# The last batch of a Fourier layer with routed experts: two queues for its loads, ACT's queue for its stores, and the last two experts' steps in plain order

## The chip, the cores and the metric

The kernel runs on one core of a Trainium2 chip. The metric is the device time of one execution in microseconds (us). TensorE is called PE in the rows (PEld is its weight load), VectorE DVE, ScalarE ACT, GpSimd POOL, SyncE SP; PEq, SPq, ACTq and POOLq are the sequencers of these engines, which issue DMA transfers. Each engine takes its own instructions in the order in which they stand in the program.

## The reference

For 8 batches of a 3136 x 256 sequence, a spectral layer is applied, and then a small expert network to the 128 rows of each batch that score highest.

```
X = rfft(x, axis=1)                       # 8 x 3136 x 256
Yr = Xr @ w_r - Xi @ w_i + b_r
Yi = Xr @ w_i + Xi @ w_r + b_i
Y = softshrink(Yr, 0.01) + 1j * softshrink(Yi, 0.01)
y = irfft(Y, n=3136, axis=1)

scores = y @ w_gate                       # 8 x 3136
for b in range(8):
    top = the 128 rows of y[b] with the highest scores[b]
    h = relu(y[b, top] @ w1)              # w1: 256 x 1024
    ye = h @ w2                           # w2: 1024 x 256
    out[b, top] = y[b, top] + sigmoid(scores[b, top])[:, None] * ye
    out[b] elsewhere = y[b]
```

## The kernel before

The transform of length 3136 is done as 98 x 32. For each batch there are five stages, all of them matmuls: `s1` (the 98-point transform; its result goes to a DRAM scratch tensor `As`), `s2` (the 32-point transform with twiddles), `spectral` (the product with the weights and the shrinkage), `s2i` (the inverse 32-point transform; its result goes to a DRAM scratch tensor `Cs`) and `s1i` (the inverse 98-point transform, whose result is the output row block). The stages of neighbouring batches run interleaved in one long loop over `t`. `s1i` runs in 16 steps a batch, `i` = 0 to 15. Two steps share one load of 98 x 1024 numbers (392 KB) from `Cs`, done by `ld_c`, and one store of the same size to `out`. For batches 0 to 6 the loaded rows are split into two parts on ACT and POOL (`split_c`, tiles `ch` and `cl`); batch 7 uses the rows as they are in one matmul (tiles `cv`, `xt` and `av`, after the three pools that its eight loads borrow). A PE result of `s1i` is copied by ACT from PSUM (tile `s`) to an SBUF tile called `ot` (two buffers) or, for some groups of batch 7, `at` (three buffers), and the store reads that tile. All of these loads and stores are issued from SP's queue. The eight loads of batch 7 are issued together, as soon as `Cs` of batch 7 is written.

Beside this runs the routing. `score` forms a batch's scores. `select` finds the 128th highest score: twelve rounds for batch 7, each of which counts on DVE (tiles `c`, `n`), sums over partitions on PE (line 258), and takes the next digit on DVE (tiles `ok`, `d`, `w`, `f`). `place` makes the list of the chosen rows (`mask`, `mt`, `row`, `hot`, and at last `idx`). Then the expert steps of one batch follow:

- `gather` (L327): POOL fetches the 128 rows of `out[b]` by an indirect DMA into `xe`. It waits until all stores of `out[b]` have landed.
- `prepare` (L335 to L343): PE transposes `xe`, DVE copies the result to `xT` (L337) and forms the gate's sum `sg` (L340), ACT takes the sigmoid `ga`.
- `hidden` (L352 to L356): 16 matmuls in two halves of 8. Each half ends in `hh` (ACT, L355) and `hl` (DVE, L356).
- `combine` (lines 227 to 229, 366 and 367): 24 matmuls into a tile named `px` (for the last batches), `ye` on DVE, and an indirect DMA on POOL that writes the 128 rows to `out[b]` (the scatter).

`fetch` and `ffn` are generators that are advanced once in each step of the loop; `fetch` runs at most two batches ahead of `ffn`. In `ffn` the last two batches are treated specially: for batch 6 the rows of batch 7 are prepared between `hidden` and `combine`, for which `ffn` waits until batch 7's `gather` has been called:

```
            if e == B * NCHK - 2:
                while len(fetched) < 2:
                    yield
                ready = prepare(*fetched[1], "m")
            combine(*item, ga, hs, tags[0])
```

The code above gives what is done; a scheduler decides the order of the instructions on each engine, and waits are placed on semaphores where data or a buffer asks for it. So an edit in one place can change the order in another.

## Time and profile before

| | |
|---|---|
| median of 3 runs | 760.71 us (760.18 to 762.15) |
| the profiled execution, its own time | 762.52 us |
| span in that execution, first to last instruction | 760.8 us |
| mean granted clock of TensorE | 0.989 |
| busy, share of the span | PE 97%, DVE 69%, ACT 64%, POOL 47% |

Times in the rows are microseconds from the start of the span. A row of a timeline gives start, duration, engine, line, operation, what it writes and reads, shape, and count; in brackets stands how long the engine had been idle before it and which event ended the wait. A PE matmul on unsplit 32-bit operands (L335, L352, L520) is shown as two passes, so "x32" there are 16 matmuls.

### The profile page before, as it was taken

The numbers are of one execution on the slowest core, as the hardware profiler recorded it, in microseconds if no ns is written. First come the engines' busy times: TensorE is split into PE (matmuls) and PEld (weight loads), VectorE is DVE, ScalarE is ACT, GpSimd is POOL, SyncE is SP. The second block draws the span as 40 slices with busy tenths as digits, with TensorE's granted clock in tenths as the row PEclk, the third lists the DMA queues.
The fourth block names the chain that finished last, engine by engine and source line by source line (L and its number), as shares of the span: only waits on it lengthen the run. The fifth ranks groups of instructions, "written<-read, shape, count | busy, mean of one in ns | idle before, by whom it ended". The sixth has DMA issues, their size and how long they took to land.

```text
span 760.8 us, 14956 instructions
## 1 busy us (share of the span) xinstructions
PE 736.0 (97%) x5232; PEld 652.9 (86%) x5232; DVE 522.5 (69%) x1413; ACT 488.1 (64%) x994; POOL 357.2 (47%) x372
## 2 busy tenths in 40 slices
PE   8799999999999999999999999999999999999987
PEld 3499989998999899999998888888999888988567
DVE  3267766665666656655898898776787799886652
ACT  2257656777787867777777768677577555455421
POOL 0345536556566655556466555565453332333101
PEclk9899999999999999999999999999999999999988
DMA  8989877888887888678767768576674364343830
GB/s 257 293 254 284 246 235 232 304 242 266 258 258 237 268 247 250 221 255 243 250 207 253 226 206 269 181 256 194 181 229 142 128 204 141 109 145 110 253 130 22
DMA packets 86224, 165.19 MB, mean 217 GB/s; under 512 B 6369, under 2 KB 58757, under 8 KB 86149
## 3 DMA queue, kind: packets, MB, share of 16 engines
q1 hardware_dynamic: 83534, 157.40, 66.1%
q0 software_dynamic: 2160, 5.60, 2.6%
q10 hardware_dynamic: 454, 1.25, 0.6%
q8 instruction: 41, 0.67, 0.4%
q14 instruction: 35, 0.28, 0.1%
HBM read 86.17 MB, written 78.12 MB: 216 GB/s over the span
## 4 chain that ended last, share of the span: by engine, by line
PE 79%; DVE 9%; DMA 6%; issue 3%; ACT 2%; POOL 0%; SPq 0%; POOLq 0%; ACTq 0%; DVEq 0%
PE py L227 11%; PE py L229 11%; PE py L228 11%; PE px L437 11%; PE s L229 9%; PE s L227 9%; PE s L228 9%; PE m L352 2%; DMA out<-ot 2%; PE s L410 2%; DMA As<-at 1%; DMA av<-As 1%; DMA xt<-in_x 1%; DVE junk L482 1%; DVE w L271 1%
## 5 line engine op out<-in xcount | busy, mean ns | idle before, releaser
L223 POOL TENSOR_TENSOR cl<-cv,ch 98x512 fp32r<-98x512 f32 x112 | 144.3, 1289 | 187.4 <-ACT ch L221 133.2
L223 POOL TENSOR_TENSOR xl<-xt,xh 98x512 fp32r<-98x512 f32 x112 | 144.4, 1291 | 92.3 <-ACT xh L221 80.3
L478 ACT COPY ct<-s 128x512 f32<-128x512 f32 (+1 forms) x104 | 59.3, 570 | 161.4 <-PE s L229 148.4
L227 PE MATMUL py<-wrh,Xh 128*128 128x256 f32 x400 | 121.8, 305 | 0.7 <-ACT Xh L440 0.7
L437 PEld LDWEIGHTS px<-g_sb,av 128*128 128x128 f32 (+1 forms) x800 | 106.3, 194 | 18.0 <-issue 5.6
L437 PE MATMUL px<-g_sb,av 128*128 128x128 f32 (+1 forms) x800 | 109.9, 280 | 4.6 <-DMA av<-As 4.2
L229 PE MATMUL py<-wrl,Xh 128*128 128x256 f32 x400 | 113.6, 284 | 0.0
L227 PE MATMUL py<-wih,Xh 128*128 128x256 f32 x400 | 113.2, 283 | 0.0
L228 PE MATMUL py<-wrh,Xl 128*128 128x256 f32 x400 | 113.2, 283 | 0.0
L228 PE MATMUL py<-wih,Xl 128*128 128x256 f32 x400 | 113.1, 283 | 0.0
L229 PE MATMUL py<-wil,Xh 128*128 128x256 f32 x400 | 112.8, 282 | 0.0
L482 DVE CUSTOM_DVE_ANT_0 junk<-s,wgb 128x256 f32<-128x256 f32 (+1 forms) x200 | 84.5, 422 | 37.6 <-ACT ct L478 34.3
L457 DVE TENSOR_TENSOR py<-py,bias 128x512 f32<-128x512 f32 (+1 forms) x104 | 70.2, 675 | 42.2 <-PE py L229 42.0
L223 DVE TENSOR_TENSOR Yl<-py,Yh 128x512 fp32r<-128x512 f32 (+1 forms) x104 | 69.4, 667 | 42.2 <-ACT Yh L221 42.1
L442 DVE TENSOR_TENSOR Xl<-px,Xh 128x512 fp32r<-128x512 f32 (+1 forms) x104 | 69.4, 667 | 28.9 <-ACT Xh L441 23.9
L459 ACT ACTIVATE r<-py,m2l 128x512 f32<-128x512 f32 (+1 forms) x104 | 70.3, 676 | 13.3 <-DVE py L457 8.6
L227 PEld LDWEIGHTS py<-wrh,Xh 128*128 128x128 f32 x400 | 75.9, 190 | 2.1 <-ACT Xh L440 1.0
L227 PEld LDWEIGHTS py<-wih,Xh 128*128 128x128 f32 x400 | 75.5, 189 | 0.9 <-issue 0.9
L228 PEld LDWEIGHTS py<-wrh,Xl 128*128 128x128 f32 x400 | 76.0, 190 | 0.1
L229 PEld LDWEIGHTS py<-wrl,Xh 128*128 128x128 f32 x400 | 75.6, 189 | 0.6 <-issue 0.5
L228 PEld LDWEIGHTS py<-wih,Xl 128*128 128x128 f32 x400 | 75.4, 189 | 0.3 <-issue 0.2
L229 PEld LDWEIGHTS py<-wil,Xh 128*128 128x128 f32 x400 | 75.5, 189 | 0.0
(153 smaller groups left out, 1748.1 us busy)
## 6 DMA issues: line engine op xcount, KB each, us to landing
av<-As SPq DMA_DIRECT2D x48, 512.0 KB
Cs<-ct SPq DMA_DIRECT2D x48, 512.0 KB
As<-at SPq DMA_DIRECT2D x60, 392.0 KB
out<-ot SPq DMA_DIRECT2D x60, 392.0 KB
cv<-Cs SPq DMA_DIRECT2D x59, 392.0 KB
xt<-in_x SPq DMA_DIRECT2D x58, 392.0 KB
gip<-t_gi POOLq DMA_DIRECT2D x6, 512.0 KB, 8.8
out<-at SPq DMA_DIRECT2D x4, 392.0 KB
```

Source lines behind the costliest of these rows:

```text
L223: track[sub] = sub.tensor_tensor(out=l, in0=src, in1=h.bitcast(F32), op=ALU.subtract).ins
L227: nc.tensor.matmul(out, wh, mh, start=start, stop=False)
L228: nc.tensor.matmul(out, wl, mh, start=False, stop=False)
L229: return nc.tensor.matmul(out, wh, ml, start=False, stop=stop).ins
L352: nc.tensor.matmul(ph[:, f, :], w1s[:, h, (4 * q + f) * 128:(4 * q + f + 1) * 128], xT[:, h, :], start=(h == 0), stop=(h == 1))
L410: nc.tensor.matmul(p, w1f, xt.pop((b, i))[:, o:o + 2, :], start=True, stop=True)
L437: nc.tensor.matmul(px[:, 2 * p + h, :], a[:, 2 * (g % 2) * (w - 1) + p, h * 128:(h + 1) * 128], g_sb[:r, 2 * g + p, :], start=True, stop=True)
L442: nc.vector.tensor_tensor(out=xl[:, :, NF:], in0=px, in1=xh[:, :, NF:].bitcast(F32), op=ALU.subtract)
L457: nc.vector.tensor_tensor(out=py, in0=py, in1=bias[:, :w, :], op=ALU.add)
L459: nc.scalar.activation(out=r1, in_=py, func=AF.Relu, bias=m2l, scale=1.0)
L478: nc.scalar.copy(out=c, in_=p)
L482: nc.vector.tensor_tensor_reduce(out=junk[:r], in0=c[:, k, :], in1=wgb[:r], scale=1.0, scalar=0.0, op0=ALU.mult, op1=ALU.add, accum_out=Cs ...
```

## The change

Three things are edited. Four of the eight loads of batch 7 (groups 1, 3, 5 and 7) are issued from ACT's queue and four from SP's. The eight stores of batch 7 are issued from ACT's queue. And `ffn` prepares each batch just before its `hidden`, batch 7 too, so that batch 6's `combine` no longer stands behind batch 7's `gather` and transposes.

```diff
@@ ld_c
-                nc.sync.dma_start(out=cv[b, k], in_=Cs[b][:, 2 * k:2 * k + 4, :])
+                q = nc.scalar if b == B - 1 and k % 4 else nc.sync
+                q.dma_start(out=cv[b, k], in_=Cs[b][:, 2 * k:2 * k + 4, :])
@@ s1i
         if i % 2 == 1:
-            nc.sync.dma_start(out=ov[b][:, 2 * i - 2:2 * i + 2, :], in_=ot[b])
+            q = nc.scalar if b == B - 1 else nc.sync
+            q.dma_start(out=ov[b][:, 2 * i - 2:2 * i + 2, :], in_=ot[b])
@@ ffn
-        ready = None
         for e in range(B * NCHK):
...
-            if ready is None:
-                ready = prepare(*item, tags[0])
-                yield
-            (xT, ga), ready = ready, None
+            xT, ga = prepare(*item, tags[0])
+            yield
             hs = []
             yield from hidden(*item[:2], xT, tags[1], hs)
-            if e == B * NCHK - 2:
-                while len(fetched) < 2:
-                    yield
-                ready = prepare(*fetched[1], "m")
             combine(*item, ga, hs, tags[0])
```

The scheduler also moves instructions that the diff does not name. Line numbers behind the edits shift by one or two (L506 becomes L507, L520 L521, L523 L524, L525 L527).

The first place is on ACT, at the start of batch 7's `s1i` steps. `ot_9939` is the tile of batch 6's last store; `ot_10009` is batch 7's first group (steps 0 and 1), `ot_10045` its second (steps 2 and 3), which uses the buffer that `ot_9939` leaves free; `at_10132` and `at_10166` are its third and fourth; `hh_10100` and `hh_10145` are the two halves of batch 4's `hidden`. Before:

```order
L523 COPY ot_10009<-s_10010 98x512
L523 COPY ot_10009<-s_10013 98x512
L355 ACTIVATE hh_10100<-py_10091 128x512
L523 COPY at_10132<-s_10133 98x512
L355 ACTIVATE hh_10145<-py_10136 128x512
L523 COPY at_10132<-s_10162 98x512
L523 COPY at_10166<-s_10167 98x512
L523 COPY at_10166<-s_10217 98x512
L523 COPY ot_10045<-s_10046 98x512
L523 COPY ot_10045<-s_10087 98x512
```

After the change the same stretch reads:

```order
L524 COPY ot_10009<-s_10010 98x512
L524 COPY ot_10009<-s_10013 98x512
L343 ACTIVATE ga_10262<-sg_10260 128x1
L527 DMA out_7<-ot_10009 98x1024
L524 COPY ot_10045<-s_10046 98x512
L524 COPY ot_10045<-s_10087 98x512
L355 ACTIVATE hh_10100<-py_10091 128x512
L527 DMA out_7<-ot_10045 98x1024
L524 COPY at_10132<-s_10133 98x512
L355 ACTIVATE hh_10145<-py_10136 128x512
```

The two copies of the second group stood behind both halves of batch 4's `hh`, and now stand ahead of them; the stores stand between the copies.

The second place is on DVE, in the middle of batch 7's `select`; the rows are named by round (`n_10007` ends round 5, `n_10029` round 6, `n_10071` round 8). The L340 rows are batch 6's gate sum, which needs batch 6's gather. Before, it stood in round 8:

```order
L248 TENSOR_TENSOR c_10069<-scores,f_10067 98x224
L340 ISA junk,sg<-xe,wgb 128x256
L340 ISA sg 128x1
L253 TENSOR_REDUCE n_10071<-c_10069 98x7
L268 TENSOR_SCALAR ok_10077<-m 98x7
```

After the change it stands two rounds earlier, behind the first `hl` of batch 4:

```order
L253 TENSOR_REDUCE n_10007<-c_10005 98x7
L356 SCALAR_TENSOR_TENSOR hl<-py,hh 128x512
L268 TENSOR_SCALAR ok_10021<-m 98x7
L340 ISA junk,sg<-xe,wgb 128x256
L340 ISA sg 128x1
L270 TENSOR_REDUCE d_10020<-ok_10021 98x1
L271 SCALAR_TENSOR_TENSOR w_10019<-d_10020,w_9997 98x1
L245 TENSOR_TENSOR f_10025<-digits,w_10019 98x7
L248 TENSOR_TENSOR c_10027<-scores,f_10025 98x224
L253 TENSOR_REDUCE n_10029<-c_10027 98x7
```

Between `ok_10021` and `c_10069` there are two more rounds, which are now behind the gate sum. On PE the round's matmul on `n_10029` now has behind it batch 4's 24 `combine` matmuls, the `s1i` steps 7 to 15, all of batch 5's `hidden` and `combine`, and batches 6 and 7.

The third place is on POOL, at the end; `idx_0_9397` is batch 4's list, then follow `9669` (batch 5), `9612` (batch 6) and `10230` (batch 7). L327 is a gather, L367 a scatter.

```order
 L367 DMA out<-ye,idx_0_7430 3136x256
+L327 DMA xe<-out,idx_0_9612 128x256
 L367 DMA out<-ye,idx_0_9397 3136x256
-L327 DMA xe<-out,idx_0_9612 128x256
 L367 DMA out<-ye,idx_0_9669 3136x256
 L327 DMA xe<-out,idx_0_10230 128x256
```

Batch 6's gather moved ahead of batch 4's scatter; batch 7's gather stays behind batch 5's scatter.

## Rows read from the trace of the kernel before

**Rows 1.** The page: busy time of each engine, its share of the span, and its instructions.

```profile
PE 736.0 (97%) x5232; PEld 652.9 (86%) x5232; DVE 522.5 (69%) x1413; ACT 488.1 (64%) x994; POOL 357.2 (47%) x372
```

**Rows 2.** The chain of work that ended last, from 690 us to the end, in order of time: start, duration, what.

```profile
700.82 3.76 DMA cv<-Cs
...
707.25 12.65 DMA out<-ot
...
720.69 4.24 DMA xe<-out,idx
```

**Rows 3.** The timeline of SP's queue from 690 us: each row is the issue of a transfer (or of two in a row).

```profile
702.28 0.33 SPq L525 DMA_DIRECT2D out<-ot  x1
...
704.48 1.68 SPq L506 DMA_DIRECT2D av<-Cs  x1
...
707.25 2.74 SPq L525 DMA_DIRECT2D out<-ot  x2
```

**Rows 4.** The timeline of ACT from 690 us.

```profile
704.21 0.58 ACT L523 COPY ot<-s 98x512 f32<-98x512 f32 x1 [1.05 <-PE s L229]
708.56 1.07 ACT L523 COPY ot<-s 98x512 f32<-98x512 f32 x2 [3.77 <-DMA out<-ot]
710.72 0.60 ACT L355 ACTIVATE hh<-py 128x512 fp32r<-128x512 f32 x1 [1.08 <-PE py L352]
...
719.98 1.07 ACT L523 COPY ot<-s 98x512 f32<-98x512 f32 x2
```

**Rows 5.** The timeline of DVE from 690 us: round 6 of `select` from `d` to the end of `n`, the round with the gate sum in it, the first `hl` of batch 4, `ye` of batch 5 and `xT` of batch 6, and batch 7's gate sum.

```profile
711.35 0.69 DVE L356 SCALAR_TENSOR_TENSOR hl<-py,hh 128x512 fp32r<-128x512 f32 x1
...
716.89 0.16 DVE L270 TENSOR_REDUCE d<-ok 98x1 uint32<-98x7 f32 x1
...
717.90 0.39 DVE L253 TENSOR_REDUCE n<-c 98x7 bf16<-98x224 bf16 x1
...
722.09 0.39 DVE L248 TENSOR_TENSOR c<-scores,f 98x224 bf16<-98x224 f32 x1
724.95 0.43 DVE L340 CUSTOM_DVE_ANT_0 junk<-xe,wgb 128x256 f32<-128x256 f32 x1 [2.48 <-DMA xe<-out,idx]
...
739.03 0.48 DVE L366 SCALAR_TENSOR_TENSOR ye<-px,ga,xe 128x256 f32<-128x256 f32 x1 [0.29 <-PE px L229]
...
740.04 0.42 DVE L337 COPY xT<-px 128x256 f32<-128x256 f32 x1
...
744.03 0.43 DVE L340 CUSTOM_DVE_ANT_0 junk<-xe,wgb 128x256 f32<-128x256 f32 x1 [3.50 <-DMA xe<-out,idx]
```

**Rows 6.** The timeline of PE from 698 us: the first `s1i` step of batch 7, the matmuls of rounds 6 and 7 (line 258), two `s1i` steps between them, the round that waited, and the last two batches' transposes and `hidden`; the last two rows are the first and the last of the 24 matmuls of batch 7's `combine`.

```profile
704.71 1.07 PE L520 MATMUL s<-cv,w1tf 98*98 98x512 f32 x2 [0.54 <-DMA cv<-Cs]
...
718.34 0.17 PE L258 MATMUL m<-n,tm 98*98 98x7 bf16 x1
...
719.29 1.94 PE L520 MATMUL s<-xt,w1tf 98*98 98x512 f32 x4
721.06 0.17 PE L258 MATMUL m<-n,tm 98*98 98x7 bf16 x1
...
725.74 0.17 PE L258 MATMUL m<-n,tm 98*98 98x7 bf16 x1 [1.85 <-DVE n L253]
...
739.57 0.44 PE L335 MATMUL px<-ident,xe 128*128 128x128 f32 x2 [0.83 <-DVE ye L366]
740.52 5.47 PE L352 MATMUL py<-xT,w1s 128*128 128x128 f32 x32 [0.52 <-DVE idx L321]
745.82 0.38 PE L335 MATMUL m<-ident,xe 128*128 128x128 f32 x2
...
748.91 3.74 PE L352 MATMUL py<-xT,w1s 128*128 128x128 f32 x32
752.41 0.36 PE L227 MATMUL px<-w2h,hh 128*128 128x256 f32 x1
...
755.35 0.28 PE L229 MATMUL px<-w2l,hh 128*128 128x256 f32 x1
```

**Rows 7.** The timeline of POOL from 690 us: L367 is a scatter, L327 a gather.

```profile
720.69 0.98 POOL L327 DMA_INDIRECT xe<-out,idx  x1 [0.49 <-issue]
739.79 0.98 POOL L367 DMA_INDIRECT out<-ye,idx  x1 [18.12 <-DVE le L318]
741.33 0.98 POOL L327 DMA_INDIRECT xe<-out,idx  x1 [0.56 <-issue]
```

**Rows 8.** The DMA queues from 5.5 to 14 us, where `ld_x` of batch 0 loads tiles of the same 392 KB from SP's queue (q1) and ACT's queue (q10) at once: MB, and the time that the packets took as a share of 16 engines' time.

```profile
DMA packets 727, 2.31 MB, mean 272 GB/s; under 512 B 83, under 2 KB 182, under 8 KB 727
...
q10 hardware_dynamic: 319, 1.16, 45.9%
q1 hardware_dynamic: 296, 1.07, 41.3%
```

**Rows 9.** The same from 708.3 to 716.9 us, where batch 7's loads come from SP's queue alone, and from 717 to 721 us, where stores follow.

```profile
DMA packets 556, 1.98 MB, mean 230 GB/s; under 512 B 73, under 2 KB 73, under 8 KB 556
...
DMA packets 344, 1.22 MB, mean 306 GB/s; under 512 B 45, under 2 KB 45, under 8 KB 344
```

**Rows 10.** Stretches of time: length, busy time and (instructions) of PE, PEld, DVE, ACT and POOL, then TensorE's granted clock (1.00 is 2.4 GHz, 0.50 is 1.2 GHz), DMA share and GB/s.

```profile
727.00:730.50 3.50, 3.50 (x19) 3.49 (x18) 2.17 (x8) 0.58 (x1) 0.00 (x0) 0.51 0.67 215
...
740.70:744.10 3.40, 3.40 (x17) 3.40 (x18) 0.07 (x1) 0.00 (x0) 1.05 (x2) 0.50 0.24 77
```

## The prediction

> **What bounds the kernel now.** Over the whole span PE is busy 97% of the time [rows 1], but the change touches only the last 60 us, so I read that stretch alone. First the chain of waits: it passes through a load of batch 7, then for 12.65 us through the landing of a store that was issued at 707.25 and seen at 719.90, then 4.24 us through batch 6's gather, and from there through batch 7's `select` and the last expert steps [rows 2]. So two things carry the end: when batch 6's last store lands, and who waits for it. The order of SP's queue names that store: its tile was copied by ACT from 704.21 to 704.79 [rows 4], but SP stood in eight loads and issued it only at 707.25 [rows 3].
>
> Then the engines' timelines, to see who waits. DVE stands still for 2.48 us, from 722.48, because batch 6's gate sum is in its order ahead of round 8's count, and the gather's rows come at 724.95; PE's matmul of that round follows at 725.74 [rows 5, 6]. ACT waits too: 3.77 us at 704.79 for a store to free the buffer of batch 7's first group, and then its copies of the second group run at 719.98, just after the last store of batch 6 was seen. But between these two ACT did `hh` of batch 4 at 710.72, and the other half later [rows 4]. So before, the late store delays a copy that nobody needs soon, and one gate sum, late in `select`. Last, TensorE's clock falls from 2.4 to 1.2 GHz at two places behind idle time of PE, from 727 to 730.5 and from 740.7 to 744.1 [rows 10]; each such stretch costs about 1.7 us of PE's work.
>
> **The change, part by part.** *When does batch 6's last store land?* Let T be the time at which it is seen; before, 719.90. Its issue comes sooner now, since SP has four loads ahead of it and not eight: at about 706 and not at 707.25, because it waits for its copy and for the first load to land (704.58, plus what sharing adds). What counts, though, is the bytes ahead of it. With loads on two queues the engines shared their time almost evenly at the start of the kernel, 1.16 MB against 1.07 MB [rows 8]. So while SP's queue moves two loads, a store and a load, ACT's queue moves its four loads, and behind these SP's last load and batch 6's last store come through. These are the same ten transfers of 392 KB as before.
>
> The Trainium skill says the same in "DMA: Bandwidth & Descriptors", section "Issuing engines are not separate DMA queues": transfers from any engine run on the same 16 DMA engines and interleave, and a second issuing engine saves only the issue time. The trace agrees (1.16 against 1.07 MB). By this rule the store lands where it did and the sum below stands; without it, with SP's queue served first, the first rival's time would come.
>
> Bounds for T: two queues moved 272 GB/s [rows 8], one queue 230 GB/s with such loads [rows 9]; eight loads of 0.40 MB take 11.8 or 14.0 us, so T is at best 2.1 us earlier, 717.8. Against that, batch 7's first store now comes on ACT's queue and does not stand behind batch 6's last one; if all its 0.40 MB pass first at 306 GB/s [rows 9], T is 1.3 us later, 721.2. I take 719.9, between them. ACT's three loads that stand ahead of a copy of batch 6 take 0.33 to 1.68 us each to issue (by SP's issues [rows 3]); even at 5 us the store would be issued at about 707, as before, so this is hidden in the queue's backlog.
>
> *Who waits for T now?* The order on ACT shows it: the copies of batch 7's second group, which need the buffer of batch 6's last store, stand ahead of both halves of batch 4's `hh`. ACT therefore stands until T. Then come two copies, 1.07 us, and `hh`, 0.60 [rows 4], and DVE's `hl`, 0.69 [rows 5], which stands in DVE's order ahead of round 6: it ends at T + 2.4. Right behind it DVE has batch 6's gate sum. The gather is now ahead of batch 4's scatter on POOL and starts at T + 0.3; from its start to the gate sum it took 4.24 us once [rows 2] and 2.70 us once (741.33 to 744.03) [rows 5, 7]. I take 2.8, since the loads and batch 6's stores are through: the rows come at T + 3.1. The gate sum takes about 0.5, the rest of round 6, from `d` to the end of `n`, 1.40 (716.89 to 718.29) [rows 5]. So PE gets round 6's count at T + 5.1 = 725.0; before it was at 718.34 [rows 6]. **Round 6 is 6.7 us late** (4.6 to 9.4 with the bounds).
>
> *From round 6 to batch 5's `ye`.* PE takes its instructions in order, and behind the matmul of round 6 stand now: 24 + 24 matmuls of two `combine`s, 3.1 us each (752.41 to 755.35 for 23 steps); nine `s1i` steps at 0.885 (two in 719.29 to 721.06), 8.0; 16 matmuls of `hidden`, 3.5 (748.91 to 752.41); one pair of transposes, 0.4; and eleven small matmuls of `select` and `place`, counted at about 0.15, 1.6 [rows 6]. That is 19.7. Added to it are a wait of about 0.5 for round 7's count (a round is longer than the 16 `combine` matmuls ahead of it) and 0.8 from the last `combine` matmul to the end of `ye` (0.29 and 0.48 [rows 5]): 21.0. PE will have stood nearly idle for some 7 us before; behind a wait of 1.85 us [rows 6] its clock fell for 3.4 us, so I add one such stretch, 1.7: 22.7. Before, the same stretch took 739.51 - 718.34 = 21.2, of which 2.5 was the stall and 1.7 the clock. **+1.5 us**, so that batch 5's `ye` ends at 747.7 and not at 739.51. The stall in round 8 is gone, as meant, but its gain is in these figures already, and what is late next is PE's own backlog.
>
> *From batch 5's `ye` to the end.* Before, this took 760.8 - 739.5 = 21.3 us. Batch 7's gather stands on POOL behind batch 5's scatter, as before (739.79, then 741.33), and its rows came at 744.03, 2 us before batch 6's `hidden` was through (740.52 + 5.47 = 745.99) [rows 5 to 7]. So batch 6's `combine` did not wait for that gather, and the edit takes away no wait. What it takes away is the cover: before, batch 7's transposes and its `xT` lay under batch 6's `combine`, and batch 7's `hidden` began at 748.91, right behind it. Now the transposes need the `px` buffer that batch 6's `ye` reads, so `ye`, transposes and `xT` come one after another between `combine` and `hidden`. The same row of steps ahead of batch 6's `hidden` took 1.78 us, 0.29 + 1.49 (739.03 to 740.52) [rows 5, 6]; 0.14 comes back, the transposes that stood ahead of batch 6's `combine` (745.82 to 745.96, where the next matmul begins). **+1.6 us**. I leave the clock as before here, one slow stretch; a second behind the new gap would cost 1.7.
>
> *Stores from ACT.* Eight issues of about 0.33 us lie between ACT's copies [rows 3]. Behind T ACT has about 1 us of work for 2 us of PE's, so they are hidden; if each held ACT for 1.68 us, ACT would set the pace of the nine steps and add up to 3 us.
>
> **The sum**, against the profiled execution's span: 760.8 + 6.7 + 1.5 + 1.6 = 770.6 us. The median of the runs shown, 760.71, is 0.1 under this span (that execution's own time, 762.52, is 1.7 over it), so I forecast **770.5 us**, 1.3% slower.
>
> **The rivals.** *The store lands early, and nobody waits.* If SP's queue were served ahead of ACT's, the store would stand behind four loads and a store alone and be seen near 712. It decides for T under about 714.5: DVE would reach round 6 at about 717.8 (716.89, plus 0.9 because the first load shares its time with the second and PE's first step, 704.71 before, starts later). Then round 6's count is at about 719.2, without idle time of PE the clock holds, and the end is 719.2 + 21.0 + 21.3 + 1.6 = 763.1 with the second slow stretch, 761.4 without it: no change. To be faster by over 0.3%, it would also need PE's backlog behind round 6 to be 3 us shorter than I count. The even shares in rows 8 speak against it; for it, that those are loads from another tensor, and that the order of issue differs.
>
> *The store is somewhat early, about 717.* Two queues at 272 GB/s or more and batch 7's first store too late to get in front: 767 to 768. This is the same mechanism with another size.
>
> *It is worse.* Batch 7's first store gets ahead (T = 721.2), the gather takes 4.24 us again, and the clock falls once more behind the new gap: 770.6 + 1.3 + 1.5 + 1.7 = 775.
>
> *The edit of `ffn` pays.* If batch 7's gather came later than batch 6's `hidden`, taking its wait away would gain what it is late. It came 2 us early, and both now move together, so I give this little.
>
> **How the numbers follow.** The forecast with its sizes (766 to 773) has a chance of 0.60, the worse case 0.10, the early store with T near 717 or below 0.10, and the case that nobody waits 0.20, which I split into 0.07 faster, 0.11 no change and 0.02 just slower. A difference of 0.3%, 2.3 us, is about what a measurement of this kernel can tell from none. That gives faster 0.07, same 0.12, slower 0.81. The range runs from 762.5, which takes in the upper end of the no-wait case, to 775.
>
> **What would show it.** ACT without an instruction from about 714 to T, and its first instruction behind that a copy of batch 7's second group; DVE waiting about 5 us or more at `hl` and the gate sum in round 6; PE nearly idle from 718 to 725; batch 6's last store still seen between 717.8 and 721.2; a slow stretch of the clock behind the idle time; and about 1.8 us between batch 6's last `combine` matmul and batch 7's first of `hidden`. The prediction is wrong if the store is seen before 714.5, if the gather's rows are there when DVE asks for them, or if PE's work behind round 6 takes much less than 21 us.

## The result, and the profile after

| | before | after |
|---|---|---|
| median, ten runs of each in turn | 764.83 us (760.18 to 769.48) | 769.11 us (766.04 to 771.59) |
| the profiled execution, own time / span | 762.52 / 760.8 us | 769.95 / 768.2 us |
| mean granted clock | 0.989 | 0.984 |

The ratio is 1.0057, with a 95% interval of 1.0031 to 1.0084: **slower, by 0.57% or 4.3 us**. The forecast was 770.5 us, slower by 1.3%. The median lies in the forecast range, but partly because the kernel before, run more often, has a median 4 us above the 760.71 that the forecast started from: executions of one program differ here by up to 9 us. The slowing itself is less than half of the one forecast (4.3 us, not 9.8). The two profiled executions differ by more than the medians do, 7.4 us by their spans; a second profile of the changed kernel, in the table by stage below, has a span of 766.6 us.

The first reading is ACT's timeline, at the start of batch 7's `s1i` steps; it answers to [rows 4].

```profile
710.80 1.07 ACT L524 COPY ot<-s 98x512 f32<-98x512 f32 x2 [5.73 <-DMA out<-ot]
...
717.76 1.07 ACT L524 COPY ot<-s 98x512 f32<-98x512 f32 x2 [5.79 <-DMA out<-ot]
718.72 0.61 ACT L355 ACTIVATE hh<-py 128x512 fp32r<-128x512 f32 x1
```

ACT waits 5.79 us for batch 6's last store, does the two copies of batch 7's second group, and only then batch 4's `hh`: at 718.72, where it was 710.72 before. The store is seen at 717.8, 2.1 us earlier than before. SP's queue and POOL show the same store from its issue to the gather that waited for it (answers to [rows 3, 7]; the last three rows are batch 5's scatter, batch 7's gather and batch 6's scatter):

```profile
706.66 0.49 SPq L527 DMA_DIRECT2D out<-ot  x1
```

```profile
717.95 0.97 POOL L327 DMA_INDIRECT xe<-out,idx  x1 [14.49 <-DMA out<-ot]
...
743.32 0.98 POOL L367 DMA_INDIRECT out<-ye,idx  x1 [15.43 <-DMA out<-at]
744.60 0.98 POOL L327 DMA_INDIRECT xe<-out,idx  x1 [0.30 <-issue]
755.49 0.98 POOL L367 DMA_INDIRECT out<-ye,idx  x1 [9.90 <-DVE ye L366]
```

DVE's timeline answers to [rows 5]: batch 4's first `hl` and batch 6's gate sum, which are both ahead of round 6; then batch 5's `ye`, batch 7's gate sum, batch 6's two `hl`, its `ye`, and batch 7's `xT`.

```profile
719.37 0.69 DVE L356 SCALAR_TENSOR_TENSOR hl<-py,hh 128x512 fp32r<-128x512 f32 x1 [0.36 <-ACT hh L355]
720.91 0.43 DVE L340 CUSTOM_DVE_ANT_0 junk<-xe,wgb 128x256 f32<-128x256 f32 x1 [0.78 <-DMA xe<-out,idx]
...
742.55 0.48 DVE L366 SCALAR_TENSOR_TENSOR ye<-px,ga,xe 128x256 f32<-128x256 f32 x1 [2.42 <-PE px L229]
...
749.08 0.42 DVE L340 CUSTOM_DVE_ANT_0 junk<-xe,wgb 128x256 f32<-128x256 f32 x1 [5.08 <-DMA xe<-out,idx]
...
749.43 0.69 DVE L356 SCALAR_TENSOR_TENSOR hl<-py,hh 128x512 fp32r<-128x512 f32 x1
...
754.73 0.48 DVE L366 SCALAR_TENSOR_TENSOR ye<-px,ga,xe 128x256 f32<-128x256 f32 x1 [3.77 <-PE px L229]
755.75 0.42 DVE L337 COPY xT<-px 128x256 f32<-128x256 f32 x1 [0.53 <-PE px L335]
```

Batch 6's first `hl` runs at 749.43 although its `hh` was done at 746.74 (ACT's row `746.14 0.60`): batch 7's gate sum stands in front of it and its rows come at 749.08. PE (answers to [rows 6]) shows what this costs, and one thing that the prediction does not name, in rounds 1 and 2:

```profile
705.36 1.52 PE L521 MATMUL s<-cv,w1tf 98*98 98x512 f32 x2 [0.91 <-DMA cv<-Cs]
706.68 0.21 PE L258 MATMUL m<-n,tm 98*98 98x1 bf16 x1
706.75 2.00 PE L521 MATMUL s<-cv,w1tf 98*98 98x512 f32 x2
708.55 0.21 PE L258 MATMUL m<-n,tm 98*98 98x7 bf16 x1
710.49 0.17 PE L258 MATMUL m<-n,tm 98*98 98x7 bf16 x1 [1.73 <-DVE n L253]
...
722.71 0.17 PE L258 MATMUL m<-n,tm 98*98 98x7 bf16 x1 [0.77 <-DVE n L253]
...
750.17 0.56 PE L228 MATMUL px<-w2h,hl 128*128 128x256 f32 x1 [2.16 <-DVE hl L356]
...
755.27 0.44 PE L335 MATMUL px<-ident,xe 128*128 128x128 f32 x2 [0.58 <-DVE ye L366]
756.23 3.84 PE L352 MATMUL py<-xT,w1s 128*128 128x128 f32 x32 [0.52 <-DVE xT L337]
```

Between the matmuls of rounds 1 and 2 (708.55 and 710.49) PE has nothing else to do, since its order has no `s1i` step there, and waits 1.73 us. The windows (columns as in [rows 10]) show TensorE's clock:

```profile
705.80:716.00 10.20, 8.47 (x20) 4.10 (x19) 5.44 (x22) 1.17 (x3) 0.00 (x0) 0.50 0.90 295
...
722.80:742.50 19.70, 19.70 (x114) 13.85 (x113) 12.20 (x52) 6.67 (x12) 1.00 (x1) 1.00 0.41 129
750.20:753.60 3.40, 3.40 (x16) 3.40 (x17) 0.69 (x1) 0.03 (x1) 0.00 (x0) 0.50 0.00 0
```

From 705.8 to 716.0 PE runs at 1.2 GHz, behind its wait of 0.91 us for the first load; behind round 6 it runs without a gap at 2.4 GHz; and it falls once more behind the 2.16 us wait for `hl`.

### The profile page after: what moved, and what is told of

Its sections match the earlier page's. It is cut to its first block, busy times and chain, and to the rows that moved or that the text cites. A ratio compares the mean times of both kernels' runs of the same rounds, so it can differ in the third digit from the quotient of the medians.

```text
span 768.2 us, 14954 instructions
## 1 busy us (share of the span) xinstructions
PE 738.9 (96%) x5232; PEld 653.9 (85%) x5232; DVE 522.8 (68%) x1413; ACT 488.3 (64%) x994; POOL 357.3 (47%) x372
## 4 chain that ended last, share of the span: by engine, by line
PE 76%; DVE 9%; issue 6%; DMA 5%; ACT 2%; POOL 1%; POOLq 0%; ACTq 0%; SPq 0%; DVEq 0%
PE py L227 11%; PE py L229 11%; PE px L437 10%; PE py L228 10%; PE s L229 9%; PE s L227 9%; PE s L228 9%; PE m L352 2%; DMA out<-ot 2%; PE s L410 2%; DMA As<-at 1%; DVE w L271 1%; DMA av<-As 1%; DVE junk L482 1%; DVE py L460 1%
## 5 line engine op out<-in xcount | busy, mean ns | idle before, releaser
L437 PEld LDWEIGHTS px<-g_sb,av 128*128 128x128 f32 (+1 forms) x800 | 106.3, 194 | 18.6 <-issue 5.7
L524 ACT COPY ot<-s 98x512 f32<-98x512 f32 x120 | 68.6, 588 | 18.7 <-DMA out<-ot 11.5
```

What stands on the lines that cost most here:

```text
L437: nc.tensor.matmul(px[:, 2 * p + h, :], a[:, 2 * (g % 2) * (w - 1) + p, h * 128:(h + 1) * 128], g_sb[:r, 2 * g + p, :], start=True, stop=True)
L524: nc.scalar.copy(out=ot[b][:, o:o + 2, :], in_=p)
```

## A table by stage

When batch 7's `scores` are ready varies from 703 to 710 us over the profiles, because the clock also has slow stretches early in the kernel, which the change doesn't touch. So the stages are counted from `scores` (DVE L498): to round 6's matmul, from there to the start of batch 5's `ye`, and from there to the end of the span. All in us, one profiled execution each; the names are those of the next sections. The last two columns are for the first two stages together: PE's idle time (their length less PE's busy time), and how long the clock was at 1.2 GHz.

| kernel | scores to round 6 | to batch 5's `ye` | to the end | sum | PE idle | half clock |
|---|---|---|---|---|---|---|
| before | 14.5 | 20.7 | 21.8 | 57.0 | 2.7 | 3.4 |
| after | 18.6 | 19.8 | 25.7 | 64.1 | 3.5 | 10.2 |
| after, profiled again | 17.9 | 19.8 | 23.0 | 60.7 | 5.0 | 3.4 |
| loads alone | 18.9 | 19.4 | 20.7 | 58.9 | 3.6 | 10.2 |
| stores alone | 22.8 | 17.1 | 20.5 | 60.4 | 6.3 | 6.9 |
| `ffn` alone | 18.0 | 20.6 | 23.6 | 62.2 | 2.8 | 6.8 and 3.4 |
| after, other buffer | 19.9 | 19.6 | 24.3 | 63.8 | 4.4 | 10.2 |
| after, gate sum late | 17.8 | 19.9 | 21.9 | 59.6 | 5.0 | 3.4 |
| after, both | 14.2 | 19.8 | 22.0 | 56.0 | 2.9 | none |
| before, gate sum late (two runs) | 18.6, 15.2 | 16.2, 16.2 | 20.3, 21.8 | 55.0, 53.1 | 0.8, 0.5 | 6.8, none |
| the same with `ffn` edit | 15.6 | 16.2 | 22.1 | 53.8 | 0.8 | none |
| the same with loads, buffer | 18.0 | 19.5 | 20.3 | 57.7 | 2.8 | 10.2 |
| the same with loads, stores, buffer | 17.9 | 19.7 | 21.9 | 59.5 | 2.9 | 10.2 |

PE runs the same 169 matmul instructions between `scores` and batch 5's `ye` in every one of these profiles, in 30.8 to 31.1 us of busy time where the clock is whole. So what the first two stages take beyond that is PE's idle time and the work done at half clock. The two profiles that can be set side by side are before and "after, profiled again", which both have 3.4 us of half clock there. PE's waits in the second:

```profile
707.37 1.07 PE L521 MATMUL s<-cv,w1tf 98*98 98x512 f32 x2 [1.14 <-DMA cv<-Cs]
...
709.78 0.17 PE L258 MATMUL m<-n,tm 98*98 98x7 bf16 x1 [0.39 <-DVE n L253]
711.64 0.17 PE L258 MATMUL m<-n,tm 98*98 98x7 bf16 x1 [1.69 <-DVE n L253]
...
723.75 0.17 PE L258 MATMUL m<-n,tm 98*98 98x7 bf16 x1 [1.69 <-DVE n L253]
```

Before, PE waited 0.54 us for the first load and 1.85 us in round 8 [rows 6]. After, the wait in round 8 is gone; there are 1.14 us for the first load, 2.1 us in rounds 1 and 2, and 1.7 us in round 6. Together these waits make up the growth of PE's idle time, 2.7 to 5.0 us.

## The experiments: the parts alone

The ratio given with each run is not the quotient of the medians, which differ from it by up to 0.16%.

**The loads alone.** Ratio 1.0010 [0.9982, 1.0038], median 766.04 us against 764.08 before.

```diff
+                q = nc.scalar if b == B - 1 and k % 4 else nc.sync
+                q.dma_start(out=cv[b, k], in_=Cs[b][:, 2 * k:2 * k + 4, :])
```

> Only the loads of batch 7 are split over two queues; stores and expert steps as before. The order then has the same two changes as the full change: ACT's copies of batch 7's second group ahead of batch 4's hh, and batch 6's gate sum in round 6. Theory W (the waits that the order puts in): +4 to +6 us against the kernel before. ACT idle until batch 6's last store is seen (about 718), round 6's count at about 723 and not 718.3. Rival Q (what costs is the time on ACT and on the DMA engines, not the order): about +1 us. Rival P (the clock: PE stands a moment for the first load and then runs at half clock for 10 us): the cost comes only with that slow stretch, and without it the time is that of before.

The loads alone bring the delay of round 6, 18.9 us behind `scores`, as in the whole change: ACT's copies of the second group wait 4.94 us for the store, `hh` comes behind them. What comes behind that is no longer than before (19.4 and 20.7 us), since the stall in round 8 is gone, and the time gives no clear loss: theory W's +4 to +6 us isn't there, and rival Q's +1 us can't be told from it.

**The stores alone.** Ratio 1.0027 [0.9999, 1.0055], median 767.26 us.

```diff
+            q = nc.scalar if b == B - 1 else nc.sync
+            q.dma_start(out=ov[b][:, 2 * i - 2:2 * i + 2, :], in_=ot[b])
```

> Only batch 7's stores are issued from ACT's queue. In this order the first hh of batch 4 stands ahead of the copies of batch 7's second group, but the second hh stands behind them, and DVE has its hl in round 5. Theory W: hl of the second half waits for batch 6's last store (about 720), round 5's count comes at about 724 and not 716.5, +4 to +7 us. Rival Q: eight issues of 0.33 us on ACT, hidden, 0 to +1 us. Rival P: no early idle time of PE, so no change.

Here a wait shows that the whole change has in another place: DVE's second `hl` of batch 4 waits 5.78 us for `hh`, which stands on ACT behind copies that wait for batch 6's last store, and PE stands:

```profile
721.46 0.69 DVE L356 SCALAR_TENSOR_TENSOR hl<-py,hh 128x512 fp32r<-128x512 f32 x1 [5.78 <-ACT hh L355]
```

```profile
723.72 0.17 PE L258 MATMUL m<-n,tm 98*98 98x7 bf16 x1 [4.69 <-DVE n L253]
```

Round 6 is 8.3 us later than before, but 3.6 us of that comes back in the next stage. PE has nearly the same work there (89 matmul instructions against 91); what is gone is most of the stall of 1.85 us in round 8 [rows 6] and the slow stretch of the clock behind it [rows 10]. So a delay of a round isn't a delay of the end of the same size. By the ratio the loss is 2 us and by the medians 3, below the 4 to 7 us of theory W.

**The edit of `ffn` alone.** Ratio 1.0024 [0.9994, 1.0055], median 766.52 us.

```diff
+            xT, ga = prepare(*item, tags[0])
+            yield
             hs = []
             yield from hidden(*item[:2], xT, tags[1], hs)
-            if e == B * NCHK - 2:
...
-                ready = prepare(*fetched[1], "m")
```

> Only the expert steps' order is changed; all transfers as before. Theory W: batch 7's gather still comes in time (744), so what shows is the lost cover alone: ye, transposes and xT between batch 6's combine and batch 7's hidden, +1.6 us, and up to +3.3 if the clock falls behind the new gap. Rival Q: 0, since no transfer moves. Rival P: +1.7 only if the profile shows a further slow stretch.

The last stage is 1.8 us longer, as theory W had it by its size, but not by the lost cover alone: batch 7's gather did not come in time, and the profile has the same picture as after: batch 7's gate sum at 747.66, and behind it batch 6's `hl` at 748.01, whose `hh` was done at 745.82. The 3.5 us in the first stage come with a half clock from 704.6 to 711.4; the edit moves nothing there.

**The whole change again.** Ratio 1.0071 [1.0038, 1.0104], median 769.61 us.

> The changed kernel once more, on the chip of the three parts. Theory W: +4 to +7.5 us, and less than the sum of the three parts, since the first two wait for the same store. Rival P: the profile shows the 10 us slow stretch near 706 again where the time is long, and not where it is short.

It repeats within its interval. By the ratios the parts add up to 0.61% and the whole is 0.57 to 0.71%; by the medians the parts add up to 7.6 us and the whole is 5.5. The parts are each too small to be told from nothing alone (about 0.3% either way), so the runs don't settle whether they add or overlap. Two profiles of the same program differ in the clock (10.2 us of half clock, from 705.8, against 3.4, from 712.8), and by 2.7 us in the last stage. So the slowing is there without the 10 us stretch, against rival P.

## The experiments: taking the waits away

**The second group on another buffer.** With an `at` buffer ACT's copies need not wait for batch 6's last store. Ratio 1.0061 [1.0037, 1.0085], median 769.72 us.

```diff
-            last_at = b == B - 1 and i // 2 % 5 > 1
+            last_at = b == B - 1 and i // 2 in (1, 2, 3, 6, 7)
```

> The whole change, and beside it batch 7's second group written to one of the three `at` buffers, so that its copies on ACT no longer wait for batch 6's last store. Nothing else is changed by hand. Theory W (the time goes where an instruction stands in line behind a wait for a transfer): ACT's copies of the second group and both `hh` of batch 4 no longer wait for T, so the first `hl` of batch 4 comes at 8 to 12 us behind `scores` and not at 15.3; batch 6's gate sum still stands on DVE ahead of round 6 and needs the gather, so the wait moves to it and grows from 0.8 us to 3 us or more, and round 6's count is 17 to 18.6 us behind `scores` (18.6 in the changed kernel, 14.5 before). The end gains 0 to 1.5 us on the changed kernel; the `hl` of batch 6 still stands behind batch 7's gate sum. Theory P (what the clock does decides, and the waits only choose where PE idles): the same time as the changed kernel within 0.3%, with 5 us or more of half clock in the tail. If the copies' wait for the store was the real cost, round 6's count falls to 15 us or less behind `scores` and the end gains 3 us or more.

Nothing is gained. ACT no longer waits for batch 6's last store, but batch 6's gate sum still stands ahead of round 6 and its gather needs the same store: it runs at 722.93, 17.6 us behind `scores` (16.8 in the change), with a wait of 1.36 us (theory W had 3 us or more). Round 6 is 19.9 us behind `scores`, later than W's 17 to 18.6; here the clock was at half for 10.2 us. Two waits for one event lay side by side, and taking one away leaves the other.

**The gate sum late.** Gate sum and sigmoid of each batch are formed in `combine`, held behind its last `hl` and `hh`. Ratio 1.0035 [1.0008, 1.0061], median 767.08 us.

```diff
@@ prepare
-        nc.vector.tensor_tensor_reduce(out=junk, in0=xe, in1=wgb[:n], scale=1.0, scalar=0.0,
-                                       op0=ALU.mult, op1=ALU.add, accum_out=sg)
-        nc.scalar.activation(out=ga, in_=sg, func=AF.Sigmoid)
@@ combine
+        with tc.issue_after(last_hl[0]):
+            nc.vector.tensor_tensor_reduce(out=junk, in0=xe, in1=wgb[:n], scale=1.0, scalar=0.0,
+                                           op0=ALU.mult, op1=ALU.add, accum_out=sg)
+        with tc.issue_after(last_hh[0]):
+            nc.scalar.activation(out=ga, in_=sg, func=AF.Sigmoid)
```

> The whole change, and beside it each batch's gate sum and sigmoid formed only behind its last `hl` and `hh`, ahead of `combine`, so that no gate sum stands on DVE or ACT ahead of a round or of a `hl`. Theory W: batch 6's `hl` follows its `hh` within 1 us and no longer stands behind batch 7's gather (3.3 us between them in the changed kernel), so that the stretch from batch 5's `ye` to the end falls from 23 to 25.6 us to 21 to 22.5; round 6 still stands behind the wait of ACT's copies for batch 6's last store, but not behind the gather, so its count comes 16 to 17.5 us behind `scores` (18.6 in the changed kernel). Together 3 to 5 us faster than the changed kernel, about the time before. Theory P: the waits move, the time stays within 0.3% of the changed kernel, and the clock's slow stretches take what the waits gave. A third way: batch 7's `hidden` is held up instead, since POOL's gather is no earlier; then the stretch from batch 5's `ye` to the end stays over 23 us with the wait at batch 7's transposes.

2.6 us less than the change with the other buffer beside it on the same chip (769.72 to 767.08). Batch 6's `hh` is at 746.25, its `hl` now right behind it, and the gate sum, asked for later, waits for nothing (lines shift here: L349 and L350 are `hh` and `hl`, L362 the gate sum, L346 `hidden`, L523 or L522 `s1i`):

```profile
746.87 0.69 DVE L350 SCALAR_TENSOR_TENSOR hl<-py,hh 128x512 fp32r<-128x512 f32 x1 [2.77 <-ACT hh L349]
...
749.27 0.42 DVE L362 CUSTOM_DVE_ANT_0 junk<-xe,wgb 128x256 f32<-128x256 f32 x1
```

The last stage is 21.9 us, against 25.7 and 23.0. So the order on DVE, not the gather by itself, made batch 6 wait for batch 7. The gain is a little under the 3 to 5 us of theory W, and round 6, at 17.8 us behind `scores`, just above its 16 to 17.5.

**Both.** Ratio 1.0012 [0.9987, 1.0037], median 764.74 us.

```diff
+            last_at = b == B - 1 and i // 2 in (1, 2, 3, 6, 7)
...
+        with tc.issue_after(last_hl[0]):
```

> The whole change with both of the other edits: the second group on an `at` buffer, and every gate sum behind its batch's last `hl`. Theory W: no instruction ahead of round 6 on ACT or DVE waits for batch 6's last store any more, so round 6's count comes 13.5 to 15 us behind `scores` (14.5 before, 18.6 in the changed kernel), PE has its work in time, and the stretch from batch 5's `ye` to the end is 21 to 22.5 us. The end is 5 to 8 us ahead of the changed kernel: as fast as before, or up to 0.4% faster. Theory P: not more than 2 us faster than the changed kernel, since the tail keeps two or three slow stretches of the clock of 3 us or more each.

Round 6 is 14.2 us behind `scores`, as before the change, and the other buffer now gives 2.3 us (767.08 to 764.74) where it had given nothing. The time is that of the kernel before, and 5.0 us under that with the other buffer alone, at the low end of what theory W had. So in the changed kernel instructions standing in line behind a wait for a transfer cost time, at both of W's places. That these waits are what the change lost does not follow, as the next run shows.

**The gate sum late, in the kernel before.** Ratio 0.9943 [0.9918, 0.9968], median 760.42 us.

```diff
@@ combine, in the kernel before
+        with tc.issue_after(last_hl[0]):
...
+        with tc.issue_after(last_hh[0]):
```

> The kernel before, with every gate sum behind its batch's last `hl` and nothing else. In its trace a gate sum made round 8 wait 2.48 us, which made PE wait 1.85 us, and the clock fell behind that for 3.4 us. Theory W: that wait is gone, and with it the slow stretch at 727 us; 2 to 3.5 us faster than before, 0.3 to 0.45%. Theory P: the wait on DVE is gone, but a slow stretch comes elsewhere in the tail, and the time is within 0.2% of before. Slower than before would mean that the wait was cover for something that then comes to the front, such as batch 7's `xT` standing ahead of the second `hl` of batch 6 on DVE.

This version beats both kernels, and by more than W expected: 4.5 us, where the wait that it takes away was 2.48 us [rows 5]. The stretch from round 6 to batch 5's `ye` falls from 20.7 to 16.2 us, since round 8 no longer waits and the clock no longer falls at 727 us [rows 10]. But this also means that the change, with the same two waits gone, is 4.3 us behind the kernel before with its one wait gone. That is the distance that the two kernels had with their waits: the kernel before paid about as much for its own, so the waits by themselves don't explain the loss.

## The experiments: what is left

**`ffn` edit on top of that.** Ratio 0.9953 [0.9927, 0.9980], median 760.42 us, beside 760.81 without it on the same chip.

```diff
@@ ffn, in the kernel before with the gate sum late
+            xT, ga = prepare(*item, tags[0])
+            yield
...
-                ready = prepare(*fetched[1], "m")
```

> The kernel before with the gate sums moved behind the last `hl`, and of the change the edit of `ffn` alone. With no gate sum in DVE's order ahead of a `hl`, what is left of the edit is the lost cover: `ye`, two transposes and `xT` one after another between batch 6's `combine` and batch 7's `hidden`. Theory C (the cover is the cost): the stretch from batch 5's `ye` to the end is 21.7 to 22.3 us, against 20.3 without the edit, and the time is 1.4 to 2 us (0.2 to 0.26%) over that of the kernel before with the gate sums moved. Theory D (the edit's cost was the gate sum in front of the `hl` alone): the same time as without the edit, within 0.1%. Against the kernel before, 0.9965 by C and 0.9943 by D.

The times don't decide between the theories: by the medians the edit costs nothing (theory D), by the ratios 0.10 to 0.16% (0.9953 against 0.9943 and 0.9937 without it), which lies between D and C. By the profile the serial row is there, and the last stage has 22.1 us against 20.3 in one profile without the edit. From batch 6's `ye` to batch 7's it is 8.4 to 8.5 us in all seven profiles with the edit and 6.6 in all seven without it, so the lost cover takes 1.8 to 1.9 us. In the other profile without the edit the last stage is 21.8 us, since the clock falls from 738.2 to 741.4 us, between batch 5's `ye` and batch 6's. Whether the serial gap is paid for by fewer such falls the runs don't settle.

**Loads, stores and other buffer on top of that.** Ratio 0.9992 [0.9966, 1.0017], median 765.15 us.

```diff
@@ the change, with the gate sum late and the buffer
-            xT, ga = prepare(*item, tags[0])
-            yield
+            if ready is None:
+                ready = prepare(*item, tags[0])
+                yield
+            (xT, ga), ready = ready, None
...
+                ready = prepare(*fetched[1], "m")
```

> Loads and stores of batch 7 as in the change, the second group on an `at` buffer, the gate sums behind the last `hl`, and `ffn` as before. Theory C: the lost cover is back, 1.4 to 2 us less than with the edit of `ffn`: 0.9985 to 0.9995 of the kernel before, with 20 to 20.7 us from batch 5's `ye` to the end. What is then left against the kernel before with the gate sums moved (0.9943), about 0.4 to 0.5%, belongs to the two queues. If instead it comes to within 0.15% of that kernel, the two queues cost nothing by themselves once nothing waits for the store, and `ffn` cost it all.

By the medians this is not faster than with the `ffn` edit (764.74 on another chip), by the ratios 0.2% faster (0.9992 against 1.0012), which is theory C's size; the intervals take in both. In the profile the cover is back, but batch 7's gather took 4.7 us, PE's transposes waited for it, and the last stage is 21.9 us, not 20 to 20.7:

```profile
749.01 0.44 PE L335 MATMUL m<-ident,xe 128*128 128x128 f32 x2 [1.49 <-DMA xe<-out,idx]
```

Against the kernel before with the gate sum late 0.49 to 0.55% is left. `ffn` is the same in both, so this belongs to the two queues, with the other buffer, which no run has by itself in a kernel with one queue.

**Loads and other buffer alone on top of that.** Ratio 0.9985 [0.9957, 1.0013], median 763.65 us.

```diff
@@ as the last one, without the stores
-            q = nc.scalar if b == B - 1 else nc.sync
-            q.dma_start(out=ov[b][:, 2 * i - 2:2 * i + 2, :], in_=ot[b])
+            nc.sync.dma_start(out=ov[b][:, 2 * i - 2:2 * i + 2, :], in_=ot[b])
```

> The same without the stores on ACT's queue: only the four loads on ACT's queue, the second group on an `at` buffer, and the gate sums behind the last `hl`. If the stores' issues on ACT cost something by themselves, this one is 0.1% or more faster than with them; if they are hidden between ACT's copies, as the prediction had it, it is the same within 0.1%. If the split loads cost what is left (through PE's longer wait for the first load, or a clock stretch behind it), it stays 0.3% or more over the kernel before with the gate sums moved; if not, it comes to within 0.15% of it.

The split loads, with the buffer, cost 2.8 us by the medians (760.81 to 763.65) and 0.48% by the ratios. The stores add 1.5 us by the medians and 0.07% by the ratios; what they cost stays open.

**The gate sum late in the kernel before, again.** Ratio 0.9937 [0.9910, 0.9965], median 760.81 us: it repeats.

> The kernel before with the gate sums moved and nothing else, a second time, beside the other three on one chip: 0.994 of the kernel before again, within 0.25%. If the first result was chance, 0.9975 to 1.

Where the split loads cost it stands in PE's busy time over 10 us, each time from 0.5 us behind `scores`, first in this kernel with one queue, then in two kernels with two (the change with both waits gone, and the loads on top of the gate sum late):

```profile
704.90:714.90 10.00, 9.73 (x52) 6.32 (x53) 6.58 (x26) 3.32 (x7) 0.00 (x0) 1.00 0.90 258
```

```profile
706.65:716.65 10.00, 7.37 (x35) 4.26 (x36) 6.64 (x29) 3.14 (x6) 0.00 (x0) 1.00 0.90 294
```

```profile
703.70:713.70 10.00, 7.39 (x13) 3.03 (x14) 4.52 (x18) 2.13 (x4) 0.00 (x0) 0.54 0.90 293
```

The transfers are faster with two queues (294 and 293 GB/s against 258), and PE does less: 52 matmul instructions with one queue, 35 with two at full clock, and 13 where the clock is mostly at half. Over the first two stages, again the kernel before with the gate sum late and then the change with both waits gone, both at full clock and with the same 169 instructions, PE idles 0.5 us and 2.9 us:

```profile
704.37:735.70 31.33, 30.81 (x169) 20.40 (x169) 22.26 (x93) 12.17 (x23) 1.97 (x2) 1.00 0.72 226
```

```profile
706.14:740.08 33.94, 31.06 (x169) 20.63 (x169) 22.81 (x96) 12.39 (x24) 1.97 (x2) 1.00 0.63 207
```

The second is 2.6 us longer, about the 2.8 us of the times, without any fall of the clock. PE's order says where. With one queue four steps and eight matmuls of `hidden` stand around the rounds up to round 2 (the kernel before with the gate sum late):

```profile
705.16 1.07 PE L522 MATMUL s<-cv,w1tf 98*98 98x512 f32 x2 [0.42 <-DMA cv<-Cs]
706.07 0.17 PE L258 MATMUL m<-n,tm 98*98 98x1 bf16 x1
706.10 1.08 PE L522 MATMUL s<-cv,w1tf 98*98 98x512 f32 x2
707.02 1.02 PE L522 MATMUL s<-xt,w1tf 98*98 98x512 f32 x2
707.88 0.17 PE L258 MATMUL m<-n,tm 98*98 98x7 bf16 x1
707.90 0.41 PE L335 MATMUL px<-ident,xe 128*128 128x128 f32 x2
708.16 1.02 PE L522 MATMUL s<-xt,w1tf 98*98 98x512 f32 x2
709.02 1.05 PE L346 MATMUL py<-xT,w1s 128*128 128x128 f32 x8
709.97 0.17 PE L258 MATMUL m<-n,tm 98*98 98x7 bf16 x1
```

With two queues, the scheduler put the steps on `xt` behind round 2, and rounds 1 and 2 stand there without cover (the rows of after above: 708.55 and 710.49, a wait of 1.73 us, which every profile with split loads has at 1.69 to 1.73, with the other buffer or without). The first load comes a little later, too (where PE waits for it, 0.91 to 1.78 us with split loads and 0.42 to 0.91 with one queue). No run keeps the order of one queue with split loads, so that the order costs this time, and not the split itself, is read from these rows and not tested. Behind this idle time the clock fell in seven of eight profiles with split loads, for 10.2 us from the first load on in five, and for 3.4 us behind round 2 in two; with one queue it fell at the first load in two of six, for 6.8 us. Where it fell for 10.2 us on top of the mended waits, round 6 is 17.9 and 18.0 us behind `scores`, where it did not it is 14.2.

Taken together: the waits that the change put in replaced a wait of the kernel before that cost about as much. Of the 4.3 us that are left with the waits gone from both kernels, the split loads, with the buffer, are 2.8 us; the other 1.5 us the runs don't divide between the stores and the edit of `ffn`.

## Why the forecast was right, and where it was not

The direction, and the mechanism of the first step, were right. Its sizes:

- **The store, T.** Taken 719.9, seen 717.8: the lower bound. The step that failed is "These are the same ten transfers of 392 KB as before", and with it that the store lands where it did. The 16 engines moved 295 GB/s here and 237 in the same window before, so the bytes went through faster. By the Trainium skill, "DMA: Bandwidth & Descriptors", section "Issuing engines are not separate DMA queues", which the prediction names for this, a second issuing engine saves only the time to issue. Here the store was issued 0.6 us earlier (706.66 against 707.25 [rows 3]) and landed 2.1 us earlier, and the measurement decides. It doesn't show that the second queue made the rate: two profiles with one queue reached 313 and 281 GB/s too (`ffn` alone from 704.6 to 711.2, and the kernel before with the gate sum late from 705.2 to 711.9), both at half clock.
- **Who waits for T.** The order was as forecast: ACT's copies, then `hh`, `hl`, the gate sum, round 6; from T to round 6's matmul 4.9 us against 5.1. Round 6 came at 722.71, 4.4 us late, not 6.7; nearly all of the miss is T. But two signs that the prediction named weren't there: DVE waited 0.36 us at `hl` and 0.78 us at the gate sum, not 5 us or more, and PE, which was to be nearly idle from 718 to 725, was busy for 6.2 of these 7 us. The step that failed is that rounds 1 to 5 come as before. Round 5's matmul was at 719.06, 2.6 us later than before (716.48), behind the waits in rounds 1 and 2 and the slow clock. A round without a wait took 1.9 us (717.16 to 719.06), so the waits for T cost round 6 some 1.8 us, and 2.7 us in the second profile (719.18 to 723.75). That the lateness of round 6 came near the forecast is in part luck. The experiments show that both waits, on ACT and at the gate sum, are real, and that taking ACT's away alone gives nothing back.
- **From round 6 to batch 5's `ye`.** +1.5 forecast, -0.9 measured (19.8 against 20.7 us). PE's work was sized well (19.7 us from 722.80 without a gap), and the waits of 0.5 us for round 7 and the slow stretch of 1.7 us weren't there. The clock had fallen already at 705.8. The step that failed is the place of that stretch.
- **From `ye` to the end.** +1.6 forecast, +3.9 measured in this profile, +1.2 in the second. The lost cover was right: 1.8 us from the start of batch 6's last `combine` matmul, 754.41, to batch 7's `hidden` at 756.23. What failed is the step that batch 6's `combine` doesn't wait for batch 7's gather. The prediction held the gather's rows against the end of `hidden` (745.99). But on DVE batch 7's gate sum stood in front of batch 6's first `hl` before the change too, and there the rows, at 744.03 [rows 5], were only 0.8 us ahead:

```profile
744.87 0.69 DVE L356 SCALAR_TENSOR_TENSOR hl<-py,hh 128x512 fp32r<-128x512 f32 x1 [0.40 <-ACT hh L355]
```

This was at half clock, with `hidden` 5.47 us long [rows 6, 10]. After, `hidden` took 3.84 us and the gather 4.4 us, not 2.7, and `hl` stood behind the gate sum from 746.74 to 749.43. The loads alone, with the expert steps as before, show the same wait with a gather of 2.8 us, 1.0 us long (`hh` done at 752.80):

```profile
753.47 0.42 DVE L340 CUSTOM_DVE_ANT_0 junk<-xe,wgb 128x256 f32<-128x256 f32 x1 [3.42 <-DMA xe<-out,idx]
753.82 0.69 DVE L356 SCALAR_TENSOR_TENSOR hl<-py,hh 128x512 fp32r<-128x512 f32 x1
```

So the edit of `ffn` took no wait off DVE: the program no longer waits for the gather there, DVE's order still does. With the gate sum late the stage is 3.7 us shorter than in this profile and 1.1 than in the second.
- **Left out.** That the split loads would change PE's order in rounds 1 and 2. In the second profile this idle time (2.1 us) stands beside that in round 6 (1.7 us). With both waits gone it is the largest cost that is left, 2.8 us by the times, with the clock's part in it.
- **The base.** The sum was made on one execution with a span of 760.8 us. Medians of 35 runs are 764.1, 764.9 and 764.9 on three chips. Against these the forecast's +9.8 would have ended at 774 to 775.

Of the rivals, "the store somewhat early" had T right (near 717), and gave 767 to 768; "nobody waits" is excluded by ACT's rows. "The edit of `ffn` pays" had its condition met, a gather later than batch 6's `hidden` (749.08 against 747.89), and still gained nothing, since `hl` waited for it on DVE.

## What to carry to other kernels

Take a wait away only after looking at what else on the path waits for the same event: here two instructions on two engines waited for one store, and taking ACT's wait away gave nothing by itself, but 2.3 us once the gate sum was out of the way. An instruction that needs a late transfer belongs in its engine's order behind everything that doesn't need it; moving the gate sum back was worth 0.6% by itself, more than any of the three edits cost alone. Before calling a wait the cause of a difference, take it out of both kernels: here the kernels stayed 4.3 us apart. And a change that speeds up transfers can lose time if the scheduler's new order leaves the matmul engine without work, as the rows suggest here: read that engine's busy time in the stretch, not the transfer's rate.

## What the runs showed of the hardware

- The clock of TensorE fell to half behind or within an idle time of PE as short as 0.71 us (the kernel before with the gate sum late, for 6.8 us), and behind 0.91 us for 10.2 us (after). It did not fall behind 0.91 us in the stores alone, nor behind 1.14 us in the second profile of after, where it fell later, for 3.4 us. Two profiles of the kernel before with the gate sum late have 6.8 us and nothing there. So the length of one idle time doesn't tell whether the clock falls, and one profile doesn't price such a stretch.
- The indirect gather of batch 7, 128 rows, took 2.7 to 2.8 us from issue to landing in six profiles and 3.2 to 4.7 us in eight. All seven with the `ffn` edit are among the slow ones, and one of the seven without it. The cause is open.

```profile
xe<-out,idx POOLq DMA_INDIRECT x1, 4.4
```

This is the issue row of that gather in the DMA view of after, from 744.30 to 750.60 us (median us from issue to landing); before, the rows of POOL and DVE give 2.70 [rows 5, 7].
